# GpSimd takes part of the last shifted reading of the exponentials in an attention and MLP block

## The chip, the core and the metric

The kernel runs on one core of a Trainium2 chip. A core has five engines with queues of their own: TensorE (PE) multiplies matrices, VectorE (DVE) and ScalarE (ACT) work on rows of up to 128 partitions, GpSimd (POOL) does simple elementwise work, and SyncE (SP) issues DMAs. Each engine runs its own list in order; an instruction that waits for another engine holds everything behind it on its own. The metric is the device time of one execution in microseconds (us), the median over several runs.

## The reference

One transformer block with adaptive normalisation, 2048 rows of 512 features in bf16. Attention has 32 heads of 16 features and no mask; the hidden width of the MLP is 1376.

```python
mod = (_silu(c) @ w_mod).reshape(c.shape[0], 6, 1, -1)     # sa, ca, ga, sb, cb, gb
h = _layernorm(x) * (1 + ca) + sa
q, k, v = heads(h @ wqkv)                                  # 32 heads of 16
p = softmax(einsum('bhqd,bhkd->bhqk', q, k) * 16 ** -0.5)
x = x + ga * (merge(einsum('bhqk,bhkd->bhqd', p, v)) @ wo)
h = _layernorm(x) * (1 + cb) + sb
x = x + gb * (gelu(h @ w1 + b1) @ w2 + b2)
```

The attention needs 32 x 2048 x 2048 exponentials, about 134 million.

## The kernel before, in words

The queries are cut into four blocks of 512 rows, and the heads into groups. The work is 32 **runs**; a run takes four heads, one block of 512 queries (in the last block eight heads and half a block), and all 2048 keys. Keys come in 16 **key tiles** of 128 rows. One key tile of one run is four **units**: the scores of one head, 128 keys by 512 queries.

A unit's scores are made on TensorE (line 798) from `kT` and the masked queries `qm`. Then there are two ways to the exponentials.

*On ScalarE.* Scores land in `st`, in groups of three units and two units in turn, and ScalarE takes the exponential into `pt` (line 847). Four matmuls side by side then multiply `pt` with the values `VEB` and add into the accumulator `od` in PSUM (line 949). A column of ones in `VEB` gives the sums of the softmax.

*On VectorE.* Scores land in `ax`. VectorE adds a constant and writes them as 16-bit integers into `ph` (line 895). Read as bf16, such an integer is two to the power of the score, with straight lines between whole powers. To smooth that, the same integers are read five times, each time with another number of `PH_SH` added, and all five readings go through the multiplication with `VEB` and are added up; softmax divides the common factor out. The first reading is `ph` itself. The other four are made by `shifts` (line 912): each is one VectorE instruction that adds a number to 2048 columns of 16-bit integers, `sh` from `ph` (line 915).

In each run key tiles 2, 6, 10 and 14 are offered to VectorE (line 286), in the first run only key tile 14; the other tiles belong to ScalarE. When ScalarE has finished its own tiles of a run and VectorE has not begun an offered one, ScalarE takes that too (`next_tile`, line 779). VectorE may work at most one run ahead of ScalarE (lines 1356 and 1357), and only from the fifth run on.

There is one accumulator `od`. When all readings of a run have been added, VectorE copies it to `OD` (line 974). `normalise` then sends the sums through DRAM to have them as columns, takes the reciprocal (line 985), spreads it to `RB`, and GpSimd multiplies `OD` by it in two pieces of 256 columns (line 1001). When a block's runs are done, `block_tail` projects, normalises, and runs the MLP for that block; its matmuls and evictions are strewn between the attention work of the next block. Projections of queries, keys and values of later groups are strewn in likewise.

What orders all this is a planner in the Python code that writes the program (`Plan`, line 100). It walks a model of the five engines in time. Each operation has an engine, a cost in microseconds written into the code, operations that it waits for, a priority, and a buffer that it takes. At each step the planner takes the operation that can start first, and among those near it the one with the best priority; `SEEDS` and `SPREAD` add a little reproducible disorder to the choice, with one seed for each 12.5 us of the plan. The result is one fixed list for each engine. Costs in the planner change no instruction, but they change the order, and by `next_tile` also how many tiles VectorE gets.

GpSimd and VectorE are kept out of each other's way: an operation marked `port` doesn't overlap in the plan with one so marked on the other engine. Shifts are marked; `ph` exps are not. GpSimd pieces (`beside`, line 1032) are placed only where VectorE does something unmarked for at least `POOL_MIN`, and `after_dve` (line 1038) makes each wait for the VectorE instruction in front of that one.

Of the kernel before, what the change touches and what calls it, by code (L numbers as in the profile page):

```python
# [12 lines left out]
ALU = mybir.AluOpType  # L13
# [3 lines left out]
I32 = mybir.dt.int32  # L17
I16 = mybir.dt.int16
# [4 lines left out]

PH_SH = (0, 20, 43, 69, 101)
NPH = len(PH_SH)


def _gain():  # L30
    tot = 0.0
    for f in range(128):
        got = 0.0
        for sh in PH_SH:
            n, m = divmod(f + sh, 128)
# [16 lines left out]
DL = 0.14  # L52
# [1 line left out]
AL = 0.21  # L54
FILL = 1.6
SPREAD = 0.3
SEEDS = (0, 961, 794, 403, 57, 861, 230, 839, 399, 786, 117, 865, 65, 827, 841, 698, 523, 583, 962, 855, 881, 719, 881, 934, 887, 31, 699, 398, 799, 61, 25, 979, 851, 389, 745, 727, 41, 947, 422, 101, 874, 307, 0, 86, 31, 93, 557, 415, 831, 0, 679, 0, 0, 0, 0, 0, 831, 123, 0, 0, 0, 0, 0, 0, 0, 0)
HEAT = 1.45


# [39 lines left out]
class Plan:  # L100
# [12 lines left out]
    def add(self, op):  # L113
        if op.todo == 0:
            self.lists[op.eng].append(op)
        return op
# [137 lines left out]
def kernel(  # L254
# [14 lines left out]
    nc = tc.nc  # L269
    P = 128  # L270
# [5 lines left out]
    QB = 512  # L276
    NQ = S // QB
    LAST = NQ - 1
# [8 lines left out]
    WIDE = 1  # L287
# [1 line left out]
    FEW = 1  # L289
    MM = 0.2155  # L290
    SPAN = (3, 2)
    POOL_US, POOL_MIN = 0.68, 0.5
    A_US = {1: 0.475, 2: 0.904, 3: 1.33}
    AHEAD = 3
    PSUM_F = 8
    FIRST_DKS, D_TIME = (14,), (0.0, 8.0, 13.0)
# [2 lines left out]
    const = ctx.enter_context(tc.tile_pool(name="const", bufs=1))  # L299
# [7 lines left out]
    def res(name, n, shape, dt, pool=work):  # L307
        return Res(name, n, lambda i: pool.tile(shape, dt, name=f"{name}{i}"))
# [4 lines left out]
    r_od = res("od", 1, [P, QB], FP32, pp)  # L313
    r_ax = res("ax", 2, [P, QB], FP32, pp)
    r_pt = [res(f"pt{n}_", NPT, [P, n * QB], BF16) for n in SPAN]
    r_ph = res("ph", 4, [P, WIDE * 4 * QB], I16)
    r_sh = res("sh", 4, [P, WIDE * 4 * QB], I16)
    r_xb = res("xb", 2, [P, TPB, D], BF16)
    r_blk = res("blk", NQ, [P, NC, D], BF16)
    r_w = res("w", 3, [P, NC, D], BF16)  # L320
# [5 lines left out]
    r_qm = Res("qm", 4, lambda i: QM[i])  # L326
# [48 lines left out]
    APR = 32  # L375
    TAIL, CB = 185, 49
    TAIL2, TAIL3 = 148, 95
    plan = Plan(dyn, later)
# [117 lines left out]
    first = {}  # L496
# [41 lines left out]
                                op0=ALU.mult)  # L538
    o_mask = op("DVE", mask, 0.6, (o_io,), prio=0.0)

    o_v0 = {}

    def v_init(v, prio, gate):
# [12 lines left out]
    def silu(o):  # L556
# [8 lines left out]
              prio=0.0, rel=(o_tr,))  # L565
# [119 lines left out]
    q_left = {}  # L685
# [14 lines left out]
            for n in range(1, 4) for p in range(2)]  # L700

    def make_q(b, cc, kind, acq):
        qm = op("NIL", None, 0.0, (), lat=0.0, prio=0.0, acq=r_qm)
        mm = proj(b, o_w[0], cc, kind, acq, after=qm)
        if (b, cc) == (0, 0):
            evs = [op("DVE", lambda o, p=p: nc.vector.tensor_scalar(
                out=qm.tile[:, p, :], in0=mm.tile[:, 0:QB], scalar1=qmask[:, p:p + 1], scalar2=None,
                op0=ALU.mult), 0.6, (mm, qm, o_mask), prio=0.1 if p == 0 else 0.45, rel=(mm,)) for p in range(2)]
        else:
            qs = op("DVE", lambda o: nc.vector.tensor_scalar(  # L710
                out=o.tile, in0=mm.tile[:, 0:QB], scalar1=QSC, scalar2=None, op0=ALU.mult), 0.6, (mm, qm),
                prio=0.3, acq=r_qs, rel=(mm,))
# [36 lines left out]
    NR = len(runs)  # L749
    HB = QB // 2  # L750
# [50 lines left out]
                         qm.tile[rows, :, hb * HB:(hb + 1) * HB], start=True, stop=True)  # L801

    def qk_deps(r, kt):
        want_q(r // 2 + 1 if r < LAST * 8 else r - LAST * 4 + 2)
        cc, par, hb = run_heads(r)
        qm, evs = o_q[(cc, runs[r][0])]
        return [evs[par or 0], o_k[(cc, kt // TPB)]], qm

    def qk_a():
# [23 lines left out]
        def go(o):  # L833
            n_a[0] += 1
            queued.append(A_US[len(got)])
            a_run[0] = got[-1][0]
# [67 lines left out]
                ph.uses -= 1  # L904

    live = {"A": 0, "D": 0}
    d_e = []

    def bits(o, k):
        return lambda: [o.tile[:, h * QB:(h + 1) * QB].bitcast(BF16) for h in range(4 * k, 4 * k + 4)]  # L910

    def shifts(r, kts, first, es):
        cols = slice(0, 4 * QB * len(kts))
        for j in range(1, NPH):
            sh = op("DVE", lambda o, j=j: nc.vector.tensor_scalar(  # L915
                out=o.tile[:, cols], in0=first.tile[:, cols], scalar1=PH_SH[j], scalar2=None, op0=ALU.add),
                0.06 + 0.54 * len(kts), es, lat=DL, prio=2.0, acq=r_sh, rel=(first,), port=True)
            sh.run = r
            for k, kt in enumerate(kts):
                pv_op(r, kt, (sh,), bits(sh, k), (sh,))  # L920

    def pv_op(r, kt, deps, srcs, owners):
        cc, par, hb = run_heads(r)

        def go(o):
            if not begun[r]:
                begun[r] = True
                pv_run[0] = r
                o_od[r] = o
# [13 lines left out]
            parts = (par,) if hb is None else (0, 1)  # L943
            for n, p in enumerate(parts):
                for i in range(4):
                    c0 = VW * (8 * cc + 2 * i + p)
                    w = QB if hb is None else HB
                    at = n * HB
                    nc.tensor.matmul(out=o_od[r].tile[32 * i:32 * i + 32, n * HB:n * HB + w],  # L949
                                     lhsT=v_tile(kt)[:, c0:c0 + 32],  # L950
                                     rhs=got[i][:, at:at + w], start=first and hb is None,
                                     stop=(left[r] == 0 and p == parts[-1]), tile_position=(0, 32 * i))
# [12 lines left out]
        plan.add(o)  # L965
# [369 lines left out]
    q_made = [0]  # L1335

    def first_run(g):
        return 2 * g if g < LAST * NC else LAST * 8 + g - LAST * NC

    def want_q(g):  # L1340
        while q_made[0] < g and q_made[0] + 1 < NQ * NC:
            q_made[0] += 1
            b, cc = groups[q_made[0]]
            due(32 + APR * (first_run(q_made[0]) - 1) - 32)
            make_q(b, cc, f"q{q_made[0]}", r_ax)
            due(1e9)
            if cc == NC - 1:
                o_h[b].uses -= 1
# [4 lines left out]
    while True:  # L1353
# [88 lines left out]
```

## Time and profile before

| what | value |
|---|---|
| median of 3 runs | 786.2 us (785.47 to 786.65) |
| the profiled execution's own time | 786.85 us |
| span in the trace, first to last instruction | 785.1 us |
| granted TensorE clock, mean | 1.000 |
| first exp on ScalarE starts | 15.4 us |
| last exp on ScalarE ends | 761.8 us |
| copies of the accumulator (line 974) | 31 |

In the rows of groups, a row gives line, engine, operation, what it writes and reads, shapes and count, then busy time in us and the mean duration in ns, then the engine's idle time just before these instructions and what ended it. Durations of neighbours on VectorE and ScalarE overlap, so the distance between two starts is less than a duration. In the rows of windows, a stretch is followed by its length and the busy time and number of instructions of each engine, then the granted clock, the share of the DMA engines and the GB/s they moved. In the rows of the timeline, start and duration in us come first, and neighbours of one kind are merged with their number behind x.

### The profile page before, as it was taken

The page shows a single profiled execution, that of the slowest core. Times are in us where ns is not written, and L with a number is a line of the kernel's source. Part 1 is how long each engine was busy: PE and PEld are TensorE (multiplying, and loading weights), DVE is VectorE, ACT ScalarE, POOL GpSimd, SP SyncE. Part 2 cuts the span into 40 slices and gives each one's busy share as a digit, 9 for nine tenths or more (in the row PEclk, how much of TensorE's full clock was granted, in tenths as well). Part 3 has the DMA queues.
Part 4 walks back from the last instruction along what each step waited for, and adds up shares of the span by engine and source line. Part 5 has one row for each costly group of instructions (what it writes and reads, how often), then busy time and mean ns, then how long its engine had stood idle before and what let it go on. Part 6 is the DMA issues. An engine that isn't in the chain of part 4 may idle for free.

```text
span 785.1 us, 20128 instructions
## 1 busy us (share of the span) xinstructions
PE 728.4 (93%) x8182; PEld 275.3 (35%) x8254; DVE 729.0 (93%) x1269; ACT 758.5 (97%) x686; POOL 101.3 (13%) x167
## 2 busy tenths in 40 slices
PE   8899999999999999999999999999888899989997
PEld 3433333333333222333233333222333444434444
DVE  6878899999999999999999999988999999999984
ACT  4999999999999999999999999999999999999994
POOL 6200103100002520010002100010001100120100
PEclk9999999999999999999999999999999999999999
DMA  7052001100011001001001010011010001000010
GB/s 215 30 168 59 18 24 43 26 15 15 15 45 49 25 19 49 18 19 44 10 20 33 24 32 7 17 33 30 25 45 24 18 18 43 20 24 18 25 44 28
DMA packets 39070, 28.19 MB, mean 36 GB/s; under 512 B 17957, under 2 KB 34374, under 8 KB 38978
## 3 DMA queue, kind: packets, MB, share of 16 engines
q1 hardware_dynamic: 38970, 26.91, 12.2%
q8 instruction: 64, 1.05, 0.6%
q14 instruction: 28, 0.23, 0.1%
q10 hardware_dynamic: 8, 0.00, 0.0%
HBM read 21.30 MB, written 2.61 MB: 30 GB/s over the span
## 4 chain that ended last, share of the span: by engine, by line
ACT 50%; PE 27%; issue 11%; DVE 10%; SPq 1%; DMA 1%; POOL 1%; POOLq 0%; DVEq 0%; ACTq 0%
ACT pt L847 47%; PE od L949 9%; PE st L798 8%; DVE sh L915 3%; DVE ph L895 3%; PE ax L1112 2%; PE ax L798 2%; ACT g L1191 1%; PE ax L1172 1%; PE ax L688 1%; SPq L716 1%; PE ax L428 1%; DVE g L1182 1%; PE t L1112 1%; PE ax L1106 0%
## 5 line engine op out<-in xcount | busy, mean ns | idle before, releaser
L847 ACT ACTIVATE pt<-st 128x1536 bf16<-128x1536 f32 x632 | 716.6, 1358 | 2.8 <-PE st L798 1.8
L895 DVE TENSOR_SCALAR ph<-ax 128x512 int16<-128x512 f32 x468 | 307.7, 681 | 15.3 <-PE ax L798 13.7
L915 DVE TENSOR_SCALAR sh<-ph 128x2048 int16<-128x2048 int16 x468 | 309.2, 691 | 2.0 <-PE od L949 1.3
L798 PE MATMUL st<-qm,kT 32*128 32x512 bf16 x1580 | 247.5, 382 | 28.9 <-ACT pt L847 22.5
L949 PE MATMUL od<-sh,VEB 128*32 128x512 bf16 (+1 forms) x2368 | 172.3, 339 | 5.4 <-DVE sh L915 3.4
L949 PEld LDWEIGHTS <-VEB 128*32 128x32 bf16 x4928 | 111.9, 95 | 161.8 <-issue 137.6
L798 PEld LDWEIGHTS <-kT 32*128 32x128 bf16 x2048 | 84.8, 91 | 235.8 <-issue 225.1
L798 PE MATMUL ax<-qm,kT 32*128 32x512 bf16 x468 | 159.8, 379 | 6.0 <-DVE ph L895 4.4
L949 PE MATMUL od<-pt,VEB 128*32 128x512 bf16 (+1 forms) x1968 | 153.6, 341 | 0.4 <-DVE OD L974 0.2
L1001 POOL TENSOR_TENSOR OT<-OD,RB 128x256 bf16<-128x256 f32 x38 | 27.9, 741 | 348.5 <-DVE sh L915 331.8
L949 PE MATMUL od<-ph,VEB 128*32 128x512 bf16 (+1 forms) x592 | 45.0, 337 | 0.0
L1172 PE MATMUL ax<-blk,W 128*128 128x512 bf16 (+1 forms) x143 | 39.5, 358 | 1.6 <-issue 0.8
L1001 POOL TENSOR_TENSOR OS<-OD,RB 128x256 bf16<-128x256 f32 x24 | 17.1, 727 | 174.8 <-DVE sh L915 154.9
L688 PE MATMUL ax<-blk,w 128*128 128x512 bf16 x100 | 32.5, 383 | 3.9 <-ACT blk L610 1.4
L1112 PE MATMUL ax<-w,g 128*128 128x512 bf16 x103 | 29.3, 381 | 1.6 <-DVE ph L895 0.8
L1182 DVE TENSOR_SCALAR g<-ax,b1c 128x512 bf16<-128x512 f32 (+1 forms) x41 | 28.3, 691 | 0.3
L594 DVE BATCH_NORM_STATS2 ln_s<-xb 128x6 f32<-128x512 bf16 x32 | 21.7, 677 | 1.2 <-DMA xb<-in_A_x_dram 1.1
L1112 PEld LDWEIGHTS <-g 128*128 128x128 bf16 x176 | 14.4, 97 | 22.3 <-issue 10.5
L974 DVE COPY OD<-od 128x512 f32<-128x512 f32 x31 | 21.2, 683 | 1.0 <-PE od L949 0.8
L1172 PEld LDWEIGHTS <-W 128*128 128x128 bf16 x176 | 13.4, 97 | 21.0 <-issue 15.5
L727 PE MATMUL ax<-w,blk 128*128 128x128 bf16 x256 | 20.3, 220 | 0.2 <-DVE ph L895 0.2
L727 PEld LDWEIGHTS <-blk 128*128 128x128 bf16 x256 | 14.8, 98 | 9.1 <-issue 8.5
(107 smaller groups left out, 331.8 us busy)
## 6 DMA issues: line engine op xcount, KB each, us to landing
RB<-rn SPq DMA_DIRECT2D x124, 64.0 KB
xb<-in_A_x_dram SPq DMA_DIRECT2D x8, 512.0 KB
out_dram<-o SPq DMA_DIRECT2D x16, 128.0 KB
qm<-qs SPq DMA_DIRECT2D x120, 16.0 KB
W<-in_B_w_dram SPq DMA_DIRECT2D x1, 1376.0 KB
w<-in_A_wqkv_dram SPq DMA_DIRECT2D x3, 384.0 KB
blk<-in_w_mod_dram SPq DMA_DIRECT2D x2, 512.0 KB
g<-in_w_mod_dram SPq DMA_DIRECT2D x2, 512.0 KB
```

The costliest lines, as they stand in the source:

```text
L594: nc.vector.bn_stats(out=st6, in_=src)
L688: return chain([(lambda ps, j=j: nc.tensor.matmul(out=ps[:, 0:QB], lhsT=w.tile[:, j, cc * P:(cc + 1) * P], rhs=o_h[b].tile[:, j, :], start ...
L727: nc.tensor.matmul(out=ps[:, t * P:(t + 1) * P], lhsT=o_h[b].tile[:, j, t * P:(t + 1) * P], rhs=o_w[2].tile[:, j, cc * P:(cc + 1) * P], st ...
L798: nc.tensor.matmul(out=o.tile[:, k * QB:(k + 1) * QB], lhsT=kT[cc][kb][rows, ko * P:(ko + 1) * P], rhs=qm.tile[rows, par, :] if hb is None ...
L847: nc.scalar.activation(out=e.tile[:, 0:len(got) * QB], in_=o.tile[:, 0:len(got) * QB], func=ACT.Exp, scale=ESC)
L895: nc.vector.tensor_scalar(out=ph.tile[:, c0:c0 + QB], in0=o.tile, scalar1=PH_B, scalar2=0.0, op0=ALU.add, op1=ALU.max)
L915: sh = op("DVE", lambda o, j=j: nc.vector.tensor_scalar(out=o.tile[:, cols], in0=first.tile[:, cols], scalar1=PH_SH[j], scalar2=None, op0= ...
L949: nc.tensor.matmul(out=o_od[r].tile[32 * i:32 * i + 32, n * HB:n * HB + w], lhsT=v_tile(kt)[:, c0:c0 + 32], rhs=got[i][:, at:at + w], star ...
L1001: two = beside(lambda c: nc.gpsimd.tensor_tensor(out=OT.tile[:, c], in0=OD.tile[:, c], in1=o5.tile[:, c], op=ALU.mult), (OT,), (OD, o5))
L1112: nc.tensor.matmul(out=ps, lhsT=g[:, f, col:col + P], rhs=rhs, start=(f == 0), stop=(f == NF - 1))
L1172: mm = chain([(lambda ps, f=f, j=j: nc.tensor.matmul(out=ps[:, 0:N], lhsT=W1[:, j, f * P:(f + 1) * P], rhs=h.tile[:, j, 0:N], start=(j == ...
L1182: ev.append(op("DVE", lambda o, f=f, mm=mm: nc.vector.tensor_scalar(out=g.tile[:, f, 0:N], in0=mm.tile[:, 0:N], scalar1=b1c[:, f:f + 1], s ...
```

## The change

Five things change.

The numbers added are now 24, 46, 70 and 104. As 70 is 24 + 46, the readings are made another way. `ph` is twice as wide. One instruction adds 24 to the first half and writes the second half; one of 4096 columns adds 46 to both halves at once and writes `sh`, which then holds readings two and three. The last reading (`last_shift`) is shared: VectorE adds 104 to the front columns, and GpSimd to the rest, in up to four pieces of 256 columns of 16 bits, taken as 128 columns of 32 bits, with 104 x 65537 added (two readings in one). The number of pieces is four, or fewer when five would be pending. The pieces are placed as `beside` places them.

The shifts of a later run don't pass those of an earlier one in the plan (`in_turn`).

All GpSimd pieces of `beside` become 128 columns instead of 256 (four for a tile of 512 columns, not two), and the planner's cost for one goes from 0.68 to 0.5.

In the planner an exp of two units costs 0.92 instead of 0.904, one of three units 1.346 instead of 1.33.

The queries of the last block are asked for somewhat earlier, and their place among masked queries is taken with another priority. The seeds differ.

```diff
-PH_SH = (0, 20, 43, 69, 101)
+PH_SH = (0, 24, 46, 70, 104)
...
-    POOL_US, POOL_MIN = 0.68, 0.5
-    A_US = {1: 0.475, 2: 0.904, 3: 1.33}
+    POOL_US, POOL_MIN = 0.5, 0.48
+    STEP_N, PMAX, LIMIT = 128, 4, 5
+    A_US = {1: 0.475, 2: 0.92, 3: 1.346}
...
-    r_ph = res("ph", 4, [P, WIDE * 4 * QB], I16)
-    r_sh = res("sh", 4, [P, WIDE * 4 * QB], I16)
+    r_ph = res("ph", 3, [P, 2 * 4 * QB], I16)
+    r_sh = res("sh", 2, [P, 2 * 4 * QB], I16)
+    r_s4 = res("sl", 2, [P, 4 * QB], I16)
...
+    step = const.tile([P, STEP_N], I32, name="step")
+    o_step = op("POOL", lambda o: nc.gpsimd.memset(step, PH_SH[-1] * 65537), 0.2, prio=0.3)
...
-        qm = op("NIL", None, 0.0, (), lat=0.0, prio=0.0, acq=r_qm)
+        qm = op("NIL", None, 0.0, (), lat=0.0, prio=0.0 if q_left else -1.0, acq=r_qm)
...
-        want_q(r // 2 + 1 if r < LAST * 8 else r - LAST * 4 + 2)
+        want_q(r // 2 + 1 if r < LAST * 8 - 2 else r - LAST * 4 + 3)
...
+    def in_turn(sh, r):
+        fn, sh.run = sh.fn, r
+        waiting[r] += 1
+        sh.gate = lambda: not any(waiting[:r])
...
+    def last_shift(r, kt, first, es, acq):
+        into = in_turn(op("NIL", None, 0.0, es, lat=0.0, prio=0.0, acq=acq), r)
+        n = max(0, min(PMAX, LIMIT - backlog[0]))
+        w = 2 * STEP_N
+        cols = 4 * QB - n * w
+        parts = [in_turn(op("DVE", lambda o: nc.vector.tensor_scalar(
+            out=into.tile[:, 0:cols], in0=first.tile[:, 0:cols], scalar1=PH_SH[-1], scalar2=None,
+            op0=ALU.add), 0.06 + 0.54 * cols / (4 * QB), [into] + es, lat=DL, prio=2.0, rel=(first,), port=True), r)]
+        for i in range(n):
+            def go(o, c=slice(cols + i * w, cols + (i + 1) * w)):
+                backlog[0] -= 1
+                after_dve(nc.gpsimd.tensor_tensor(
+                    out=into.tile[:, c].bitcast(I32), in0=first.tile[:, c].bitcast(I32), in1=step, op=ALU.add))
+            backlog[0] += 1
+            parts.append(op("POOL", go, POOL_US, [into, o_step] + es, lat=0.1, prio=0.6, kind="beside", rel=(first,),
+                            port=True, gate=lambda: plan.beside(POOL_MIN)))
+        pv_op(r, kt, parts, bits(into, 0), (into,))
...
     def shifts(r, kts, first, es):
-        cols = slice(0, 4 * QB * len(kts))
-        for j in range(1, NPH):
-            sh = op("DVE", lambda o, j=j: nc.vector.tensor_scalar(
-                out=o.tile[:, cols], in0=first.tile[:, cols], scalar1=PH_SH[j], scalar2=None, op0=ALU.add),
-                0.06 + 0.54 * len(kts), es, lat=DL, prio=2.0, acq=r_sh, rel=(first,), port=True)
-            sh.run = r
-            for k, kt in enumerate(kts):
-                pv_op(r, kt, (sh,), bits(sh, k), (sh,))
+        kt, n = kts[0], 4 * QB
+
+        def add(j, dst, src, us, deps, acq=None):
+            o = op("DVE", lambda o: nc.vector.tensor_scalar(
+                out=dst(o), in0=src(), scalar1=PH_SH[j], scalar2=None, op0=ALU.add),
+                us, deps, lat=DL, prio=2.0, acq=acq, rel=(first,), port=True)
+            return in_turn(o, r)
+        one = op("NIL", None, 0.0, es, lat=0.0, prio=0.0)
+        a = add(1, lambda o: first.tile[:, n:2 * n], lambda: first.tile[:, 0:n], 0.6, [one])
+        b = add(2, lambda o: o.tile, lambda: first.tile, 1.14, [a], r_sh)
...
+        last_shift(r, kt, first, [one], r_s4)
...
-        return [op("POOL", lambda o, c=c: after_dve(fn(slice(c * HB, (c + 1) * HB))), POOL_US, deps, lat=0.1,
+        return [op("POOL", lambda o, c=c: after_dve(fn(slice(c * P, (c + 1) * P))), POOL_US, deps, lat=0.1,
                    prio=prio, kind="beside", rel=rel, port=True, gate=lambda: plan.beside(POOL_MIN))
-                for c in range(2)]
+                for c in range(QB // P)]
...
-            due(32 + APR * (first_run(q_made[0]) - 1) - 32)
+            due(32 + APR * (first_run(q_made[0]) - 1) - (32 if b < LAST else 48))
```

More of the change, by code (lines that the diff above doesn't have):

```diff
@@ L56 @@
 SPREAD = 0.3
-SEEDS = (0, 961, 794, 403, 57, 861, 230, 839, 399, 786, 117, 865, 65, 827, 841, 698, 523, 583, 962, 855, 881, 719, 881, 934, 887, 31, 699, 398, 799, 61, 25, 979, 851, 389, 745, 727, 41, 947, 422, 101, 874, 307, 0, 86, 31, 93, 557, 415, 831, 0, 679, 0, 0, 0, 0, 0, 831, 123, 0, 0, 0, 0, 0, 0, 0, 0)
+SEEDS = (861, 0, 121, 999, 511, 342, 209, 0, 758, 703, 299, 529, 754, 102, 946, 0, 786, 430, 206, 610, 501, 0, 918, 431, 383, 277, 250, 387, 989, 571, 147, 971, 257, 0, 830, 493, 33, 595, 543, 225, 59, 693, 882, 69, 0, 346, 570, 606, 603, 0, 628, 0, 0, 153, 0, 991, 969, 0, 0, 0, 0, 0, 0, 0, 0, 0)
 HEAT = 1.45
@@ L906, with go @@
     live = {"A": 0, "D": 0}
+    waiting = [0] * NR
+    backlog = [0]
+    def in_turn(sh, r):
+        fn, sh.run = sh.fn, r
+        waiting[r] += 1
+        sh.gate = lambda: not any(waiting[:r])
+        def go(o):
+            waiting[r] -= 1
+            if fn is not None:
+                fn(o)
+        sh.fn = go
+        return sh
+    def last_shift(r, kt, first, es, acq):
[15 more added lines that the diff above has]
+        pv_op(r, kt, parts, bits(into, 0), (into,))
     d_e = []
@@ L912, in shifts @@
     def shifts(r, kts, first, es):
-        cols = slice(0, 4 * QB * len(kts))
-        for j in range(1, NPH):
-            sh = op("DVE", lambda o, j=j: nc.vector.tensor_scalar(
-                out=o.tile[:, cols], in0=first.tile[:, cols], scalar1=PH_SH[j], scalar2=None, op0=ALU.add),
-                0.06 + 0.54 * len(kts), es, lat=DL, prio=2.0, acq=r_sh, rel=(first,), port=True)
-            sh.run = r
-            for k, kt in enumerate(kts):
-                pv_op(r, kt, (sh,), bits(sh, k), (sh,))
+        kt, n = kts[0], 4 * QB
[7 more added lines that the diff above has]
+        b = add(2, lambda o: o.tile, lambda: first.tile, 1.14, [a], r_sh)
+        first.uses += 1
+        pv_op(r, kt, (a,), bits(first, 1), (first,))
+        first.uses -= 1
+        pv_op(r, kt, (b,), bits(b, 0), (b,))
+        pv_op(r, kt, (b,), bits(b, 1), (b,))
+        last_shift(r, kt, first, [one], r_s4)
     def pv_op(r, kt, deps, srcs, owners):
```

## The prediction

> **What bounds the kernel now.** I read the page's busy shares, then its groups, then windows of the trace cut at the copies of the accumulator (line 974), which close the 32 runs.
>
> ```profile
> PE 728.4 (93%) x8182; PEld 275.3 (35%) x8254; DVE 729.0 (93%) x1269; ACT 758.5 (97%) x686; POOL 101.3 (13%) x167
> ```
>
> ScalarE (ACT) is the fullest, VectorE (DVE) and TensorE (PE) are close behind, GpSimd (POOL) is nearly empty. The groups say what fills them:
>
> ```profile
> L847 ACT ACTIVATE pt<-st 128x1536 bf16<-128x1536 f32 x632 | 716.6, 1358 | 2.8 <-PE st L798 1.8
> L895 DVE TENSOR_SCALAR ph<-ax 128x512 int16<-128x512 f32 x468 | 307.7, 681 | 15.3 <-PE ax L798 13.7
> L915 DVE TENSOR_SCALAR sh<-ph 128x2048 int16<-128x2048 int16 x468 | 309.2, 691 | 2.0 <-PE od L949 1.3
> L949 PE MATMUL od<-ph,VEB 128*32 128x512 bf16 (+1 forms) x592 | 45.0, 337 | 0.0
> ```
>
> See: 632 exps fill 716.6 us with 2.8 us of idle before them. They are 316 of three units and 316 of two, 1580 units in all, so a unit (128x512 scores) costs 716.6/1580 = 0.4535 us. VectorE did 468 units, 117 key tiles of four. Offered were 31 runs x 4 + 1 = 125. Matmuls that read `ph` number 592 = 86x4 + 31x8 (a last-block tile takes eight): the last block lost 1 tile, the others 7. A tile that VectorE does not reach goes to ScalarE and costs 4 x 0.4535 = 1.81 us there. All eight are worth 14.5 us; the change has no other way to take exps off ScalarE.
>
> The windows show why tiles are lost: columns are length, then busy time of PE, PEld, DVE, ACT, POOL.
>
> ```profile
> 72.10:143.60 71.50, 65.61 (x674) 23.30 (x677) 61.79 (x107) 71.50 (x64) 14.21 (x20) 1.00 0.11 28
> 254.00:276.10 22.10, 19.97 (x201) 6.50 (x203) 22.00 (x37) 22.10 (x21) 11.65 (x18) 1.00 0.09 23
> 362.00:385.30 23.30, 22.09 (x205) 7.17 (x206) 23.12 (x39) 23.30 (x22) 1.46 (x2) 1.00 0.11 36
> 481.30:504.50 23.20, 22.18 (x206) 6.85 (x209) 23.16 (x39) 23.20 (x22) 1.45 (x2) 1.00 0.07 17
> 504.50:535.40 30.90, 28.60 (x230) 8.90 (x233) 23.95 (x40) 30.84 (x25) 2.92 (x3) 1.00 0.10 28
> 668.00:690.90 22.90, 21.14 (x311) 9.17 (x314) 22.76 (x38) 22.90 (x21) 1.98 (x3) 1.00 0.08 18
> ```
>
> By the `od<-pt` matmuls between two copies of `od`, eight runs have 13 `pt` tiles instead of 12: runs 2, 3, 4 (the first row), 10, 15, 20, 21 and 28 (one row each). In runs 10, 15, 20 and 28 VectorE idles 0.04 to 0.2 us: there it is VectorE's time that loses the tile. In runs 2 to 4 it idles 9.7 us and in run 21 7.0 us: there something else does (projections of the other head groups; the long GELU on ScalarE). Between 50.7 and 762 us PE idles 45 us and spends 16.7 us on zero matmuls from `warm`. So ScalarE sets the end, and VectorE sets how much ScalarE must do.
>
> How a GpSimd instruction stands beside VectorE:
>
> ```profile
> 78.35 0.68 DVE L895 TENSOR_SCALAR ph<-ax 128x512 int16<-128x512 f32 x1
> 78.51 0.73 POOL L1001 TENSOR_TENSOR OT<-OD,RB 128x256 bf16<-128x256 f32 x1 [43.55 <-DVE sh L915]
> ...
> 79.72 0.69 DVE L895 TENSOR_SCALAR ph<-ax 128x512 int16<-128x512 f32 x1
> 79.87 0.72 POOL L1001 TENSOR_TENSOR OT<-OD,RB 128x256 bf16<-128x256 f32 x1 [0.63 <-DVE sh L915]
> 80.32 1.43 DVE L915 TENSOR_SCALAR sh<-ph 128x2048 int16<-128x2048 int16 x2
> ```
>
> GpSimd starts 0.16 us after the `ph` exp. The shift that starts 0.60 us after that exp meets its last part: the pair of shifts takes 1.43 us, where undisturbed neighbours start 0.60 us apart and a pair takes 1.28. So 0.15 us is lost, and a GpSimd piece shorter than about 0.73 - 0.15 = 0.58 us would cost nothing.
>
> **The change, part by part.** Prices are starts to starts, since neighbours overlap.
>
> *Shifts.* Removed per tile: four of 128x2048, 4 x 0.60 = 2.40 us. Added: one of 2048 (0.60); one of 4096; and a rest of 2048 - 256n columns for n GpSimd pieces. The 4096 form is not in the trace. Above, it is two shifts, 1.20. Below, line 605 (128x512 bf16, SBUF to SBUF) starts every 0.32, so a column costs at least (0.60 - 0.32)/1536 = 0.00018 and 4096 cost 0.97. I take 1.12, nearer the shift's own row, since line 605 has other operands. The rest with n = 3 (1280 columns) lies between 0.60x1280/2048 = 0.375 and 0.60 - 768x0.00018 = 0.46; I take 0.40. Sum 2.12, a saving of 0.28 us a tile (0.14 to 0.45 with the ends), or 117 x 0.28 = 33 us of VectorE.
> [...]
>
> *Why n = 3.* [...] There are 468 `ph` exps and about 165 others (lines 594, 974, 1182, 1155, 1203, 710, 620), some 630. Normalising and scaling weights take, now in pieces of 128 columns, 31x4 + 17x4 = 192. What remains is 440 for 117 tiles, 3.8 each at perfect packing; the code offers fewer when five are pending.
>
> *A piece's price.* 256 columns take 0.67 (line 1024, bf16) to 0.73 us; 128 columns on 4 partitions (line 558) took 0.42. So 0.42 to 0.73; I take 0.45, as line 558 has the same number of columns. That is under 0.58, so nothing is lost to the next shift; and the 34 shifts that now run long (5.1 us over their usual time, from the trace) are mostly freed, as normalising is cut to the same size.
>
> *New order on VectorE.* The 4096-wide shift reads what the 2048-wide one wrote. Standing back to back it must wait for its end, 0.12 us beyond the usual step (a shift behind the `ph` it needs: 0.72 against 0.60). From 0 to 117 x 0.12 = 14 us; I take 4, since the list mostly has exps to put between. Later on PE's queue: the last reading's matmuls now wait for pieces that run beside the next tile's exps, 2 to 5 us later. Behind them stand all later matmuls of that queue, `st` for ScalarE among them; the two spare `pt` sets and reordering cover it, else ScalarE idles (a rival).
>
> *Spending it.* Relief 33 + 5 - 4 = 34 us. Each tile won costs VectorE 4x0.60 + 2.12 = 4.52 us and 1.81 us of shorter run. Four tiles (runs 10, 15, 20, 28) take 25 us; the one of run 21 takes 6.3, beside 7.0 us idle there. PE pays for a tile four more groups of four matmuls at 0.23 (eight in 0.62 us, four in 0.39) and about 0.5 for single score matmuls, 1.4; five tiles take 7 + 9 = 16 us of its 62. Three tiles of runs 2 to 4 I leave out. So 5 x 1.81 = 9.1 us.
>
> *At no cost.* The `step` memset lies in the 15.4 us before the first exp, where POOL is busy 10.3. The earlier queries of the last block move eight small DMAs each (line 716) about 16 x 0.45 = 7 us up SP's queue, ahead of normalising's transfers; nobody waits long for those as two `OD` buffers stand behind them. GpSimd's own late work, the reciprocal root (lines 599, 601), can stand behind a piece, 0.45 us x 16, in front of `z` for which VectorE waits 4.6 us in all: a few us at worst, under VectorE's other work. Buffers: three `ph` of double width for four. The dearer exp in the planner's costs (2.266 a pair, where the trace has 716.6/316 = 2.268) changes no instruction, but with the seeds it reorders all. Bounds: usual steps of exps are 1.330 and 0.904, means 1.347 and 0.923, so late starts cost 316 x 0.036 = 11 us; a better order could win that, a worse one lose as much. I take 0.
>
> The sum stands against the profiled execution: 786.85 us, of it span 785.1 and 1.75 outside; the median of the runs shown, 786.2, is 0.65 lower. Forecast: 786.2 - 9.1 = 777.1.
>
> **Rivals.**
> *All eight tiles, or fewer late exps*: 786.2 - 14.5 = 771.7, down to 760 if all late starts go too. For it: at n = 4 the rest is some 0.06 shorter, 7 us more relief, and VectorE's idle time in runs 2 to 4 is 9.7 us. Against: that idle time shows VectorE was not what lacked there.
> *TensorE takes the gain.* It is 93% busy, and runs 20 and 28 leave it 1.0 and 1.8 us idle; a tile asks 1.4 + 1.8. Against: zero matmuls and 45 us idle elsewhere. Result 782 to 787, around 784.5.
> *The change does little*: pending pieces hold n at 0 or 1, the rest at 0.60 to 0.53. Relief 117x0.09 + 5, two tiles: 782.6.
> *Late pieces hold the accumulator, slower.* Place: a run's last reading, line 949 before line 974; only one `od` exists, so the next run's matmuls wait. Price: if the pieces come one exp, 0.60 us, too late for each of 31 ends, 18.6 us: 786.2 - 9.1 + 18.6 = 795.7. It decides from 9.1/31 = 0.29 us a run. For it: no spare `od`; `od` waits for shifts 14 times already (3.4 us). Against: twelve to thirteen exp tiles per run can be ordered between.
> *Pieces too long, slower.* [...] At 0.73 us a piece, 3 x 117 x 0.15 = 53 us of VectorE eat the relief of 34: four tiles lost, 786.2 + 7 = 793. It decides from 0.58 us. Against: line 558.
>
> **How the numbers follow.** Forecast 0.42 (own range 773 to 782); all eight or better 0.18; TensorE 0.16, of which 0.07 within 0.2%; little 0.04; late pieces 0.15; long pieces 0.05. Faster by over 0.2% (under 784.6, about what can be told from no change): 0.42 + 0.18 + 0.09 + 0.04 = 0.73; same 0.07; slower 0.20. Below 768 I put 0.08, above 792 0.10: range 768 to 792.
>
> **What would show it.** Right: line 847 near 1560 units (707 us), `ph` exps 488, a 4096-wide shift stepping 1.1, GpSimd int32 pieces of 0.45 us, some 350, no shifts over 0.75 us. Wrong: ScalarE idle before line 847 for PE, or PE waiting on POOL for `od`; pieces above 0.58; exps still near 1580.

## The result, and the profile after

The changed kernel takes 784.47 us in the median (782.85 to 787.64, 22 runs), the kernel before beside it 786.51. The ratio is 0.9971, with a 95% interval of 0.9959 to 0.9983: faster, but by 2.3 us where 9.1 were forecast. The profiled execution has a span of 783.3 us against 785.1, and what is read from profiles below is one execution of each kernel.

Groups of the profile after (line, engine, operation, out and in, count, then busy time, mean ns, idle before):

```profile
PE 740.1 (94%) x8384; PEld 272.2 (35%) x8384; DVE 720.3 (92%) x1194; ACT 749.2 (96%) x677; POOL 291.3 (37%) x641
...
L852 ACT ACTIVATE pt<-st 128x1536 bf16<-128x1536 f32 x623 | 707.6, 1323 | 7.7 <-PE st L803 6.5
L900 DVE TENSOR_SCALAR ph<-ax 128x512 int16<-128x512 f32 x492 | 322.5, 684 | 18.9 <-PE ax L803 15.3
L938 POOL TENSOR_TENSOR sl<-ph,step 128x128 int32<-128x128 int32 x377 | 173.8, 463 | 325.8 <-DVE sh L953 99.1
...
L953 DVE TENSOR_SCALAR sh<-ph 128x4096 int16<-128x4096 int16 x123 | 150.1, 1222 | 0.6 <-PE od L994 0.4
...
L953 DVE TENSOR_SCALAR ph<-ph 128x2048 int16<-128x2048 int16 x123 | 84.0, 685 | 0.4
L932 DVE TENSOR_SCALAR sl<-ph 128x1024 int16<-128x1024 int16 (+4 forms) x123 | 59.0, 483 | 3.4 <-PE od L994 2.3
```

The work moved as planned. VectorE made 492 score exps, 123 tiles, six more than before; ScalarE lost 24 units. GpSimd did 377 pieces, 3.07 a tile, of 0.463 us each. Yet the busy time of ScalarE's exps fell by 9.0 us only, where 24 units at their usual steps are worth 10.7, and its idle time before them rose from 2.8 to 7.7 us.

To find where the gain went I split the span by the starts of ScalarE's instructions. An exp that has its scores in time starts 1.330 us behind a three-unit exp and 0.904 behind a two-unit one; what a start is later than that is called a **late start** here. It contains the idle time and also the short waits that a busy share doesn't show. The lines of the table add up to the span within 0.3 us.

| us | before | after | difference |
|---|---|---|---|
| until the first exp starts | 15.4 | 18.8 | +3.4 |
| exps at their usual steps | 705.9 | 695.2 | -10.7 |
| late starts | 11.1 | 18.1 | +7.1 |
| ScalarE's other work between (GELU, table loads) | 29.2 | 27.8 | -1.4 |
| after the last exp | 23.2 | 23.0 | -0.2 |

So the 10.7 us came, and 10.5 of them went again: a third before the first exp, two thirds where exps start late. The first exps, before and after (start, duration, engine, line):

```profile
15.44 1.45 ACT L847 ACTIVATE pt<-st 128x1536 bf16<-128x1536 f32 x1 [0.49 <-PE st L798]
...
18.82 1.45 ACT L852 ACTIVATE pt<-st 128x1536 bf16<-128x1536 f32 x1 [0.49 <-PE st L803]
```

In the kernel before, 29 starts were late by more than 0.12 us (6.9 us together), in the changed one 44 (13.8 us). Two places of this second kind stand out. In these windows the columns are length, busy time of PE, PEld, DVE, ACT, POOL, then the granted clock, the share of the DMA engines and GB/s:

```profile
126.20:129.60 3.40, 2.95 (x35) 1.24 (x34) 3.37 (x9) 3.40 (x4) 1.15 (x3) 1.00 0.02 5
129.60:133.00 3.40, 3.31 (x27) 0.81 (x29) 2.55 (x7) 2.52 (x4) 1.51 (x4) 0.50 0.24 78
...
238.80:242.20 3.40, 2.23 (x23) 0.34 (x19) 2.26 (x6) 3.17 (x4) 1.19 (x3) 1.00 0.08 20
242.20:245.60 3.40, 3.40 (x28) 1.77 (x27) 2.90 (x5) 1.98 (x2) 0.17 (x1) 0.50 0.31 81
```

In each pair the matmuls of the first stretch are, by an estimate, about a third of what TensorE does in such a time with full ones (0.33 and 0.31; the last section says how this is counted), though the engine counts as busy for 87 and 66% of it. In the second stretch it is granted half its clock, and ScalarE idles 0.9 and 1.4 us. The profiled execution of the kernel before has no such stretch between its start and its end.

How much half clock an execution has can be had from its mean granted clock, as 2 x (1 - clock) x span, as these two profiles show a granted clock of 1.00 or 0.50 and nothing between. Over 31 executions of the changed kernel (the 22 here and 9 of after_again) it is 6.2 us in the mean, and a us of it goes with 0.30 us more of span; over 114 executions of the kernel before beside the experiments it is 3.0 us, at 0.29. Drawn to a whole clock (an estimate), the spans are 784.5 us before and 781.2 after. So about 1 us of what is missing goes with the clock, and the rest does not. Which of the two comes first, a late exp or the half clock, this doesn't show.

### The profile page after: what moved, and what is told of

The parts are those of the page before. It is cut to its first block, busy times and chain, and to the rows that moved or that the text cites. A ratio compares the mean times of both kernels' runs of the same rounds, so it can differ in the third digit from the quotient of the medians.

```text
span 783.3 us, 20916 instructions
## 1 busy us (share of the span) xinstructions
PE 740.1 (94%) x8384; PEld 272.2 (35%) x8384; DVE 720.3 (92%) x1194; ACT 749.2 (96%) x677; POOL 291.3 (37%) x641
## 4 chain that ended last, share of the span: by engine, by line
PE 31%; ACT 30%; DVE 25%; issue 8%; DMA 2%; POOL 2%; SPq 1%; POOLq 0%; DVEq 0%; ACTq 0%
ACT pt L852 29%; PE od L994 12%; DVE ph L900 10%; PE st L803 9%; DVE sh L953 4%; PE ax L1157 3%; PE ax L1217 3%; DVE ph L953 2%; PE ax L803 2%; DVE sl L932 2%; DVE ln_s L599 2%; DMA dc<-dn 1%; DMA xb<-in_A_x_dram 1%; PE ax L693 1%; SPq L721 1%
## 5 line engine op out<-in xcount | busy, mean ns | idle before, releaser
L900 DVE TENSOR_SCALAR ph<-ax 128x512 int16<-128x512 f32 x492 | 322.5, 684 | 18.9 <-PE ax L803 15.3
L938 POOL TENSOR_TENSOR sl<-ph,step 128x128 int32<-128x128 int32 x377 | 173.8, 463 | 325.8 <-DVE sh L953 99.1
L953 DVE TENSOR_SCALAR sh<-ph 128x4096 int16<-128x4096 int16 x123 | 150.1, 1222 | 0.6 <-PE od L994 0.4
L994 PE MATMUL od<-ph,VEB 128*32 128x512 bf16 (+1 forms) x1240 | 90.9, 340 | 1.5 <-DVE ph L953 0.8
L994 PE MATMUL od<-sh,VEB 128*32 128x512 bf16 (+1 forms) x1240 | 85.1, 340 | 2.0 <-DVE sh L953 1.5
L953 DVE TENSOR_SCALAR ph<-ph 128x2048 int16<-128x2048 int16 x123 | 84.0, 685 | 0.4
L932 DVE TENSOR_SCALAR sl<-ph 128x1024 int16<-128x1024 int16 (+4 forms) x123 | 59.0, 483 | 3.4 <-PE od L994 2.3
L1046 POOL TENSOR_TENSOR OT<-OD,RB 128x128 bf16<-128x128 f32 x76 | 35.6, 471 | 62.6 <-DVE sh L953 28.5
L994 PE MATMUL od<-sl,VEB 128*32 128x512 bf16 (+1 forms) x620 | 50.1, 343 | 0.7 <-DVE sl L932 0.4
L1046 POOL TENSOR_TENSOR OS<-OD,RB 128x128 bf16<-128x128 f32 x48 | 21.9, 455 | 27.9 <-DVE sh L953 15.2
```

The source lines that it names most:

```text
L900: nc.vector.tensor_scalar(out=ph.tile[:, c0:c0 + QB], in0=o.tile, scalar1=PH_B, scalar2=0.0, op0=ALU.add, op1=ALU.max)
L932: parts = [in_turn(op("DVE", lambda o: nc.vector.tensor_scalar(out=into.tile[:, 0:cols], in0=first.tile[:, 0:cols], scalar1=PH_SH[-1], sca ...
L938: after_dve(nc.gpsimd.tensor_tensor(out=into.tile[:, c].bitcast(I32), in0=first.tile[:, c].bitcast(I32), in1=step, op=ALU.add))
L953: o = op("DVE", lambda o: nc.vector.tensor_scalar(out=dst(o), in0=src(), scalar1=PH_SH[j], scalar2=None, op0=ALU.add), us, deps, lat=DL, p ...
L1046: two = beside(lambda c: nc.gpsimd.tensor_tensor(out=OT.tile[:, c], in0=OD.tile[:, c], in1=o5.tile[:, c], op=ALU.mult), (OT,), (OD, o5))
```

## The experiments

### Is it the dearer exp? The two parts, each in lists chosen alike

A planner's list hangs on its seeds, and those of the two kernels had been chosen for each. So I took the two ways of the shifts and the two costs of an exp apart and chose the seeds anew for each of the four, by one procedure.

```diff
-SEEDS = (0, 961, 794, ...)
+SEEDS = (chosen anew, the same way for each of the four kernels)
-    A_US = {1: 0.475, 2: 0.904, 3: 1.33}
+    A_US = {1: 0.475, 2: 0.92, 3: 1.346}      # only in old_dear and new_dear
```

> The kernel before with seeds chosen anew: window by window 32 candidates, kept where the planner's list ended first; the same search, with the same effort, gives the seeds of the other three kernels of this set, so that the four differ in the way of the shifts (old, new) and in the planner's cost of an exp (cheap: 0.904 and 1.33; dear: 0.92 and 1.346) and not in how well the seeds suit them. Both theories: it stands near the kernel before, 785 to 792 us.

> The old way of the shifts, only the planner's exp one per cent dearer, seeds by the same search. Theory A (the dearer exp spends the gain: the planner takes the exp to end later than it does and puts other matmuls ahead of its scores, so exps start late): fewer exps than old_cheap, but no faster, 0 to 5 us slower. Theory B (TensorE has no room for the tiles won, whatever the planner believes): same time as old_cheap within 2 us, late exps only where tiles were won. The prediction's own reading (VectorE's time loses the tiles): same number of exps as old_cheap.

> The new shifts with GpSimd's pieces, the planner's exp left at 0.904 and 1.33, seeds by the same search. Theory A: the gain of the pieces comes out, 5 us or more below old_cheap and below new_dear, late starts of exps near the 11 us of before. Theory B: within 2 us of old_cheap and of new_dear, with about as many exps as old_cheap. The prediction's reading: some 9 us below old_cheap.

> The changed kernel with seeds by the same search (its first loads are issued in the old order). Theory A: 3 to 8 us slower than new_cheap, about 18 us of late starts. Theory B: within 2 us of new_cheap. The prediction's reading: some 9 us below old_dear, with 24 units fewer on ScalarE.

A second, independent choice of seeds came later:

> The kernel before with another independent choice of seeds (32 candidates a window). If the loss of the changed kernel sits in its one list: lists scatter by several us, and this one stands some 5 to 9 us above new_2, as old_cheap and old_dear stood above new_cheap and new_dear (4.6 and 11.2). If the change itself brings 2 us and no more: within 3 us of new_2.

> The changed kernel with another independent choice of seeds (40 candidates a window). Loss in the one list: 783 to 788, 5 to 9 us under old_2, with 14 to 20 us of late starts. Loss in the change: within 3 us of old_2.

| kernel | median us | ratio to the kernel before (95%) | exps | usual steps | late starts | half clock | late starts there |
|---|---|---|---|---|---|---|---|
| old_cheap | 794.01 | 1.0097 (1.0084 to 1.0110) | 634 | 707.7 | 17.9 | 17.1 | 5.9 |
| old_dear | 796.67 | 1.0155 (1.0118 to 1.0193) | 629 | 702.4 | 21.4 | 13.7 | 7.7 |
| old_2 (cheap) | 794.33 | 1.0086 (1.0058 to 1.0114) | 632 | 705.9 | 23.9 | 23.9 | 11.8 |
| new_cheap | 789.44 | 1.0047 (1.0030 to 1.0065) | 631 | 704.2 | 16.1 | 6.8 | 3.0 |
| new_dear | 785.44 | 0.9986 (0.9969 to 1.0003) | 626 | 698.8 | 13.1 | 0 | 0 |
| new_2 (dear) | 788.22 | 1.0018 (0.9998 to 1.0037) | 626 | 698.8 | 18.4 | 6.8 | 1.3 |

The columns from exps on are those of the profiled execution, in us but for the count; the last one is what starts are late inside stretches of half clock and in the 3 us behind them.

Theory A falls: with the new shifts the dearer exp is faster by 4.0 us, with the old ones slower by 2.7, and no rule can be read from it. Theory B falls as well: all three lists of the new way stand below all three of the old way, 787.7 against 795.0 in the mean, 7.3 us. In the profiles 4.7 us are exps that ScalarE need not do, and 5.2 are fewer late starts; the first exp comes 0.7 us later in the mean. The lists of one way differ by 2.7 to 4.0 us among themselves, so 7.3 is known to a few us only, and new_2 had 40 candidates a window where the others had 32.

The clock has a share in this that must be taken off. Outside stretches of half clock the new lists' exps start no less late than the old ones' (13.1, 13.1 and 17.1 us against 12.0, 13.7 and 12.1): all of the 5.2 lies where the clock is halved, and of that the old lists have more. Over the 46 executions of the six kernels, a us of half clock goes with 0.34 us of span. Drawn to a whole clock by this (an estimate), the spans are 787.1 to 788.3 us for the old lists and 781.5 to 786.1 for the new ones, 3.6 apart in the mean. Why the old lists lose more clock was not tried.

The groups of old_cheap and new_dear show the same kind of exp, fewer of them and less idle time in front:

```profile
L847 ACT ACTIVATE pt<-st 128x1536 bf16<-128x1536 f32 x634 | 718.8, 1360 | 9.3 <-PE st L798 5.4
```

```profile
L852 ACT ACTIVATE pt<-st 128x1536 bf16<-128x1536 f32 x626 | 709.3, 1343 | 4.2 <-PE st L803 2.5
```

What follows: between lists chosen alike the change is worth 7 us, but only about half of that is left at the same clock, and the 4.7 us of spared exps account for it. A gain of 9.1 us by spared exps, as forecast, these lists don't show: they win fewer tiles than the changed kernel's own list. And the change was measured against a list that fits well. The kernel before stands 7 to 10 us below lists of its own kind, and 2.5 to 4 below their spans at a whole clock, where its own is 784.6 in the mean of 47 executions; the changed kernel's list stands 1 to 5 us below lists of its kind, and its 18.1 us of late starts are no better than theirs.

### The first exp, and the halved clock

Four kernels were run on one chip, the changed one among them. `first` issues the two halves of the first input block ahead of the first weight load; `zeros` adds six groups of zero matmuls in the two places.

```diff
+            for _ in range({92: 1, 93: 1, 94: 1, 191: 3}.get(n_a[0], 0)):
+                zeros(pv_run[0])
...
         def go(o):
+            halves()          # both loads of the first block, if not yet issued
             first[i] = nc.sync.dma_start(out=o.tile, in_=wm_src[:, :, i * D:(i + 1) * D])
```

> The changed kernel as it is, beside the next three on the same chip: 784.5 us, ratio 0.997; first exp near 18.8 us, one or two stretches of 3.4 us at half the TensorE clock.

> All lists of the changed kernel as they are, only the two halves of the first input block are issued ahead of the first weight load, as the kernel before has them. Theory C (the seed of the first 12.5 us put the weights first, and the first exp starts 3.4 us later for it): first exp near 15.5 us, 3 us off the total, 781.5. Theory D (what is late in the middle sets the time, the start is caught up): within 1 us of the changed kernel.

> All lists of the changed kernel as they are, with six more groups of zero matmuls in the two places where TensorE's work falls to about a third of a 3.4 us stretch and its clock then halves (one behind each of the score groups 92, 93 and 94, three behind score group 191). Theory E (the halved clock makes the exps behind it late): no half clock in the record, ScalarE without its idle time at 132 and 242 to 246 us, 2.5 to 4 us off the total, 781. Theory F (those exps are late for the matmuls ahead of them, at any clock): no gain, or up to 1 us lost by the added matmuls.

> The order of the first loads and the zero matmuls together. C and E together: 6 to 7 us off the changed kernel, 777.5 to 778.5, ratio near 0.989. D and F: 784.

Measured: after_again 784.32 us (0.9977, 0.9968 to 0.9986), first 785.16 (0.9982, 0.9970 to 0.9993), zeros 784.86 (0.9980, 0.9964 to 0.9995), both 784.10 (0.9975, 0.9965 to 0.9986). Nothing moved.

In the profiles of `zeros` and `both` the clock is whole from the first exp to the last (1.000 and 0.999 in the mean of the span), and late starts are 16.6 us. But after_again, without a zero matmul more, has 16.4, and no halved clock at the two places either: the one stretch it has lies at 21.4 us. So the halved clock comes in some executions and not in others: with the zero matmuls, too, four of the 12 executions of `zeros` have a mean of 0.996. In the profile after it goes with 3.7 us of late starts, and that execution's span is 1.4 us longer than the one of after_again. Theory E holds for an execution that has it, but adding the zero matmuls gains nothing in the median: executions of `zeros` at a whole clock have spans of 781.7 to 783.5 us, where 781.2 was estimated above for the changed kernel, so what the clock gives back the added matmuls seem to take.

In `first` the first exp still starts at 18.3 us. Its inputs came 1.1 us earlier (normalisation statistics at 4.15 instead of 5.21), but VectorE's list had the copy of the modulation columns ahead of the first normalisations. `start` moved that copy behind them as well.

> The changed kernel, with the first input block loaded ahead of the weights and, on VectorE, the copy of the modulation columns (line 588) moved behind the four first normalisations (line 610) instead of ahead of them; all else in the lists stays. Theory C, mended: the first exp starts near 15.5 us instead of 18.6 and the total falls by 3 us, to 781.5. Theory D (the middle catches up or loses it again): under 1 us.

> The same, with the six groups of zero matmuls of the earlier run. C: 3 us, and 0 to 1.5 us more for the clock that isn't halved: 780 to 781.5. D: 784.

Measured: start 786.45 us (0.9983, 0.9969 to 0.9998), start_zeros 784.31 (0.9966, 0.9953 to 0.9979), the first exp at 18.4 and 18.7 us. The timeline of `start` shows what held it now (start, duration, engine, line):

```profile
8.85 2.16 DVE L624 TENSOR_SCALAR z<-xb,mv,rs 128x512 bf16<-128x512 bf16 x3 [0.69 <-POOL rs L620]
...
9.23 0.94 PE L580 MATMUL ax<-sc,blk 128*128 128x1 bf16 x32
...
10.03 0.38 PE L435 MATMUL od<-warm 128*128 128x512 bf16 x1
...
11.55 0.59 PE L430 MATMUL ax<-warm 128*128 128x512 bf16 x2
...
13.07 0.38 PE L430 MATMUL ax<-warm 128*128 128x512 bf16 x1
...
13.29 1.05 PE L673 MATMUL st<-ident,z 128*128 128x128 bf16 x16
...
18.35 1.45 ACT L873 ACTIVATE pt<-st 128x1536 bf16<-128x1536 f32 x1 [0.49 <-PE st L824]
```

The normalised block is ready at 11.0 us, and its transposes (L673) start at 13.29: between the modulation columns (L580) and them, TensorE's own list has zero matmuls, from 10.0 to 13.1 us. Presumably the planner put them there because in its clock the block came later. `start2` leaves them out.

```diff
+    def at_start():
+        h = heat()
+        if h is not None and 8.0 < plan.now < 11.6:
+            h.fn = lambda o: None
+        return h
-    plan.heat = heat
+    plan.heat = at_start
```

> Run start once more, and the 14 zero matmuls that the planner placed between 8.0 and 11.6 us left out; they stand in TensorE's list between the modulation columns and the first transposes and took 10.0 to 13.1 us there. Theory C: first exp near 15.5 us, 3 us off the changed kernel, 781.5, ratio 0.993. Theory D: first exp near 15.5, but under 1 us off in the end, as the middle is held by something else.

> The same with the six groups of zero matmuls that keep the clock. C: 780 to 781.5. D: 784.

Measured: start2 781.10 us (0.9927, 0.9914 to 0.9940), start2_zeros 781.71 (0.9943, 0.9925 to 0.9961). In the timeline of start2 the transposes follow the columns, and the first exp comes 2.9 us earlier than in the changed kernel:

```profile
9.08 0.95 PE L586 MATMUL ax<-sc,blk 128*128 128x1 bf16 x32 [0.21 <-DMA blk<-in_w_mod_dram]
...
10.63 1.01 PE L679 MATMUL st<-ident,z 128*128 128x128 bf16 x15 [0.53 <-DVE z L630]
...
15.88 1.45 ACT L879 ACTIVATE pt<-st 128x1536 bf16<-128x1536 f32 x1 [0.49 <-PE st L830]
```

Theory C holds: those 3 us go through to the end, 784.3 to 781.1 (on two chips; 3.9 by the ratios), and the middle takes nothing back (late starts 17.8 us). This kernel is faster than the kernel before and the changed one. Three things were mended in it, loads, VectorE's order and TensorE's list; the first alone and the first two together gained nothing, as the next queue held the same exp. Whether TensorE's list could have been mended without the other two was not tried.

### Which engine do the late exps wait for?

Four kernels keep every list and take work off one engine. The short diffs, for the changed kernel:

```diff
# pe_after: the two readings of the 4096-wide shift (light), a quarter of the columns
                     w = QB if hb is None else HB
+                    if light and not first and left[r] > 0:
+                        w //= 4
...
# dve_after: the 4096-wide shift over 2048 columns
-        b = add(2, lambda o: o.tile, lambda: first.tile, 1.14, [a], r_sh)
+        b = add(2, lambda o: o.tile[:, 0:n], lambda: first.tile[:, 0:n], 1.14, [a], r_sh)
...
-        pv_op(r, kt, (b,), bits(b, 1), (b,))
+        pv_op(r, kt, (b,), bits(b, 0), (b,))
```

> All lists of the changed kernel, but the matmuls of the readings two and three (the 4096-wide shift's) run over a quarter of their columns, so part of the sum is left out; waits and order stay. TensorE has some 123 x 2 x 0.16 = 39 us less to do. Theory G (the exps that start late wait for a full TensorE): late starts fall from 16 to 18 us to under 11, 5 us or more off the changed kernel. Theory H (they wait for VectorE's long instructions: the accumulator's copy, the score exps): late starts stay above 14, under 3 us off.

> The same for the kernel before: the matmuls of its readings two and three over a quarter of their columns (part of the sum is left out), lists unchanged, 37 us off TensorE. Theory G: it gains less than the changed kernel does, 2 to 4 us of its 11 us of late starts. Theory H: 0 to 3 us, as the changed kernel.

> All lists of the changed kernel, but the 4096-wide shift is done over 2048 columns only, and reading three repeats reading two; 123 x 0.53 = 65 us off VectorE, no order changed. Theory G: under 3 us off the changed kernel, late starts above 14. Theory H: 4 to 8 us off, late starts under 11.

> The same relief for the kernel before: its shifts two and three over 1024 columns each, the matmuls read these twice; 117 x 0.54 = 63 us off VectorE, lists unchanged. Theory G: under 3 us off the kernel before. Theory H: 3 to 6 us off. If this gains as much as the changed kernel does under the same relief, what is late is no matter of the change.

With less work for TensorE both kernels became slower than they were, or no faster: pe_after 786.94 us (0.9997, 0.9967 to 1.0028, where the changed kernel has 0.9971) and pe_before 791.28 (1.0064, 1.0037 to 1.0092). Neither theory had that. In the profiled executions the mean granted clock fell to 0.976 and 0.983, with seven and six spells of half clock where the profiles of the full kernels have two and none; late starts rose to 23.3 and 16.7 us. One such stretch of pe_after, where ScalarE idles 1.0 us (columns as before):

```profile
265.00:270.40 5.40, 4.60 (x55) 1.56 (x47) 5.40 (x9) 5.40 (x6) 2.41 (x6) 1.00 0.18 52
270.40:280.60 10.20, 10.20 (x54) 1.89 (x53) 8.52 (x13) 9.21 (x9) 3.08 (x7) 0.50 0.03 6
```

The clock can be taken out by comparing executions that were granted the same. At a mean clock of 0.991 the spans of pe_after are 782.7 and 782.8 us, those of the changed kernel 784.6 to 785.5 (four executions); at 0.993 it is 781.6 against 785.1 and 785.9; at 0.996, 780.4 against 782.9 to 784.5. For pe_before it is 786.2 against 786.8 and 787.1 at 0.993. So at the same clock the lighter matmuls, an estimated 39 us less for TensorE (123 x 2 x 0.16, three quarters of the step of 0.215 us), are worth 2 to 4 us in the changed kernel and about 1 in the old one; the loss comes with the clock. Late starts say the same: outside the halved stretches and the 3 us behind them, 11.1 us remain in pe_after and 14.4 in the changed kernel.

With an estimated 65 us less for VectorE (123 x 0.53, the step of 1.13 us less that of 0.60; its busy time falls by 54): dve_after 780.95 us (four executions; 0.9924, 0.9894 to 0.9953), 3.4 below after_again or 4.2 by the ratios; dve_before 785.62 (0.9976, 0.9962 to 0.9991), about 1.3 to 1.9 below the kernel before. At a clock of 0.998 the spans of dve_after are 779.1 and 779.3 us, those of the changed kernel 781.7 to 782.7. So VectorE's time, or the length of its instructions, holds some 3 us in the changed kernel and less in the old one; late starts are 14.1 and 11.3 us. Theory H asked for 4 to 8 us and late starts under 11, G for under 3 from VectorE and 5 or more from TensorE: neither holds. Each engine holds about 3 us, and with either relieved most late starts stay. That leaves the order in the lists as what makes them late, which is argued here and not shown: which operations would have to change places was not tried, nor both reliefs at once.

Two such places can be read in the profile after. At 239 us VectorE waits for the sums of the softmax to come back from DRAM, and TensorE for VectorE:

```profile
239.98 0.25 DVE L1030 RECIPROCAL dc<-dc 128x16 f32<-128x16 f32 x1 [1.14 <-DMA dc<-dn]
...
241.29 0.37 PE L803 MATMUL ax<-qm,kT 32*128 32x512 bf16 x1 [1.16 <-DVE ph L900]
...
241.92 1.02 ACT L852 ACTIVATE pt<-st 128x1024 bf16<-128x1024 f32 x1 [0.23 <-PE st L803]
```

The load of those sums was issued at 236.61 us; VectorE's list has the instruction that needs them ahead of the score exps. And in the last block, TensorE waits four times for the copy of the accumulator (L985, L1019):

```profile
PE st L803 <- ACT pt L852: 16.8, 56, 0.8
PE ax L803 <- DVE ph L900: 4.4, 14, 1.2
PE od L985 <- DVE OD L1019: 1.8, 4, 0.7
```

Behind these waits exps start late by 1.07 (at 581), 0.82 (625), 0.46 (742) and 0.42 us (600). No wait of TensorE for GpSimd's pieces stands in that view.

## Why the prediction was wrong

**Right.** The bound (ScalarE's exps), the only way to shorten it (tiles moved to VectorE), and nearly every price. One column each, forecast and measured from starts: first shift 0.60 and 0.60; 4096 columns 1.12 and 1.13; the rest at 1280 columns 0.40 and 0.40; pieces a tile 3 and 3.07; a piece 0.45 and 0.463. That makes 2.13 us a tile with three pieces, where 2.12 was said. A piece beside a score exp cost the next shift nothing that can be told: the shift starts 0.60 us after the exp with a piece beside the exp and without one, and one 2048-wide shift of 123 lasts over 0.75 us.

**Tiles.** Five were forecast, six came: the five named and the one of run 3; runs 2 and 4 still lose theirs. The term is 10.7 us instead of 9.1, right but for its size.

**Where it failed.** The step is the last one under "At no cost": "with the seeds it reorders all ... I take 0". The bounds were stated (11 us either way) and the middle taken; measured is +7.1 us of late starts. The other half of the same step is the start: the 15.4 us before the first exp were taken as fixed, with only the memset put there, while the first seed had also changed. It cost 3.4 us, and start2 shows that 3 of them are real at the end. The forecast without these two is 786.2 - 10.7 - 1.4 = 774; with them 784.6. Of the 7.1 us some 2 go with the 6.8 us of half clock that this execution had (at 0.30 us each, an estimate); the sum of the prediction had no term for a clock that falls. What makes the other 5 late stays open.

**Rivals.** "TensorE takes the gain" named 784.5 us, within 0.1 of the result, but its mechanism is at most a part: the six tiles ask TensorE for about 19 us by the prediction's own prices, and taking an estimated 39 us off it gives 2 to 4 us back at the same clock, of the 7 that went; relieving VectorE gives as much. "Late pieces" is not borne out: no wait of TensorE for a piece stands in the profile. But its place, the single accumulator between two runs, does cost late exps in the last block, by VectorE's copy. "Pieces too long" and "the change does little" are excluded by 0.463 us and 377 pieces. The range, 768 to 792, held the time, though not for its reasons; the likeliest case's own, 773 to 782, did not.

**What stays open.** Why the list of the kernel before fits so well and keeps its clock, and which part of the late starts belongs to which pair of instructions. That the list moves the time by as much as the change does is shown by six lists; the sequence of causes within one was only read, not tested, except at the start.

## What to carry to other kernels

When a change also redraws a whole schedule, forecast the work and the schedule as two terms: here the work came as its prices said (10.7 us of exps), and the redrawn schedule took 10.5 of it back. A schedule tuned for one kernel should be compared with one tuned as long for the other, and executions with the same granted clock with each other: of the 7.3 us between lists chosen alike, about half went with the clock. And look at the start-up by itself: what stood in the queues ahead of the first exp went almost one to one into the total, and mending one queue showed nothing while the next held the same 3 us.

## What the runs showed of the hardware

Taking matmul work away cost time in pe_before, and the clock went with it: with an estimated 37 us less of it (117 x 2 x 0.16), it took 791.28 us where the kernel before beside it took 786.92, and the mean granted clock of its profiled execution was 0.983. In these traces TensorE's granted clock falls to 0.50 for stretches of 3.4 us, or two or three of these, after a stretch in which it did little, even where the profile calls it 66 to 87% busy. How little it did is an estimate: each matmul counts by its columns and by its share of the largest form in the traces, 128 rows by 128 columns (32 rows or 32 columns are a quarter), against a stretch full of that form (512 columns in 0.215 us, its step in the profile after). So counted, the two stretches ahead of the drops in the profile after have about 0.33 and 0.31, the least of that whole profile. Over all the traces here 31 of 38 drops came behind stretches at or under 0.375, the others up to 0.42; and a few stretches as low kept their clock (0.33 at 295 us in start2_zeros). A us at half clock goes with 0.29 to 0.34 us of span in these kernels. The drops change place from one execution to the next: the profile after has them at 129.6 and 242.2 us, that of after_again, the same kernel, has one at 21.4. What sets them off is not shown here.

GpSimd's 32-bit adds of 128 columns take 0.463 us each in the profile after, in the mean of 377, and a score exp takes 0.683 us beside one and 0.685 with GpSimd idle.
